# A decode-attention kernel: masks filled by GpSimd, and the output projection in column blocks of 64

## The chip, the cores and the metric

The kernel runs on one core of a Trainium2 chip. The core has a matrix engine (TensorE, "PE" in the profile; "PEld" is its weight loading), a vector engine (VectorE, "DVE"), an activation engine (ScalarE, "ACT"), a general engine (GpSimd, "POOL"), and a queue engine (SyncE, "SP") that issues most transfers. Sixteen DMA engines carry the transfers. The metric is the device time of one execution in microseconds; smaller is better.

## The reference

One decode step for eight sequences (B = 8, one new token each, D = 512):

```python
xn = layernorm(x)
q = (xn @ wq)                         # 32 heads of 128
k = k_cache[:, :, Sk - W:, :]         # 8 key/value heads, window W = 1024 of 4096
v = v_cache[:, :, Sk - W:, :]         # each shared by 4 query heads
p = softmax(q @ k^T * 128**-0.5)
s = (p @ v).reshape(8, 1, 4096) @ wo  # 4096 -> 512
g = silu((gelu(xn @ w_gate) * (xn @ w_up)) @ w_down)   # F = 1792
out = x + s * g
```

All inputs are bfloat16. The windows of the two caches are 16.8 MB each, wq and wo 4.2 MB each, and the three feed-forward matrices 1.8 MB each: about 47 MB are read once, and 8 KB are written.

## The kernel before

The kernel is written in an order fixed by hand; each engine works through its instructions in program order and waits on semaphores for others.

Loads. Nearly all go through SyncE's queue in one order: wq in three pieces, the gate and up matrices, keys and values of the eight heads alternately (K three heads ahead), the down matrix among them, and at the end wo in five pieces. They land in a pool of nine large buffers (`big`), so that a load is issued when the buffer it takes has been read by its last reader. A cache load of one head is 2 MB. wo comes as `pieces`: row blocks m = 0 and 1 together, m = 2, then m = 3 in three cuts of 4, 3 and 1 row groups.

Start. GpSimd fills identity matrices and zeroed tiles (`zeros`, `quarter`, `sums`, `oL`, L156 to L248). The new tokens are normalised, the query projection runs (L305), and the queries are turned. `spread_x` puts x into the layout of the output. The gate and up products follow (L355), and between them `masks()` builds four masks on VectorE from the identity matrix: `parts` and `gsel` by reductions; `own`, the score mask read by L461; `same`, read by L477; and `sums`, the row-summing weights of L541.

Attention. For each of 16 sets s (a head and half of the sequences) there are steps spread over the loop: transposition of keys by TensorE (L431) with copies out of PSUM by VectorE (L442) and ScalarE (L444), the scores (L453), masking and maxima (L461, L472, L477), exponentials (L486), a turn of the probabilities (L493), and the product with the values (L519). For each head, `gather` (L541) sums the partial rows and `divide` (L550, L553) normalises; for each pair of heads, `turn_pair` (L568) transposes the result into `oL`. The steps of the feed-forward part are put between them; `fold` and `gate` end it.

Output. A transposed pair m holds 8 row groups r. The 512 output columns are cut into blocks; `spread` and `project` compute block q = NG * s + g into partition group g of a PSUM tile (partitions 32g to 32g + 31), and they shift the weights by s columns so that row b * NS2 + s of that group holds sequence b. With NG = 2 and NS2 = 2 there are four blocks of 128 columns. `oL` has a row pitch of `OL + 1`, and a read shifted by s takes its place from that odd pitch. Since a head's result holds each sequence PB = 4 times, `turn_pair` writes four copies of a pair; with NS2 = 2 a pair owns two of the places, and the other two lie in the places of the next pair, which writes them anew later.

End. Two VectorE operations multiply by the gate and add x (L675, L676); two stores, one from ScalarE's queue (L680) and one from SyncE's (L681), write the 8 KB of output.

Of the kernel before, what the change touches and what calls it, by code (L numbers as in the profile page):

```python
# [11 lines left out]
BF16 = mybir.dt.bfloat16  # L12
FP32 = mybir.dt.float32
# [4 lines left out]
def kernel(  # L18
# [13 lines left out]
    nc = tc.nc  # L32

    B, Sq, D = A_x.shape
    Hkv, Sk, Dh = A_k_cache.shape[1], A_k_cache.shape[2], A_k_cache.shape[3]
# [8 lines left out]
    P = nc.NUM_PARTITIONS  # L44
# [17 lines left out]
    NQB = D // 128  # L62
    PB = 32 // B

    NG = 2
    NS2 = NQB // NG
    NEG = -1.0e30


# [5 lines left out]
    small = ctx.enter_context(tc.tile_pool(name="small", bufs=3))  # L75
    rows = ctx.enter_context(tc.tile_pool(name="rows", bufs=1))
# [4 lines left out]
    ps_s = ctx.enter_context(tc.tile_pool(name="ps_s", bufs=1, space=PSUM))  # L81
# [6 lines left out]
    m_top = m_ps[:, 0:P]  # L88
# [3 lines left out]
    x_sb = rows.tile([B, D], BF16, name="x_sb")  # L92
# [48 lines left out]
    for k0, cuts in ((0, (1, 1)), (2, (2,))):  # L141
        t = big.tile([P, 2, Hq * Dh], BF16, name="big")
        i = 0
        for n in cuts:
            nc.sync.dma_start(  # L145
                out=t[:, i : i + n, :],
                in_=A_wq.rearrange("(p k) n -> p k n", p=P)[:, k0 + i : k0 + i + n, :],
# [10 lines left out]
    def select(out, in_, op, fill, base, pattern, cm):  # L158
# [8 lines left out]

    sizes = (2 * NS * 2 * NC, NDC * 32, NDC * 32, 32 + NS2)
    zeros = rows.tile([P, sum(sizes)], BF16, name="zeros")
# [16 lines left out]
        out=xhat, in0=x_sb, scalar1=mv[:, 0:1], scalar2=rstd[:, 0:1],  # L186
# [6 lines left out]
    for k in range(NDC):  # L193
# [4 lines left out]
        out=xqT.rearrange("p k (y g) f -> p k g y f", y=NB)[:, :, :, :, 0],  # L198
        in_=xnT_ps.rearrange("p k (g y) -> p k g y", y=NB),
# [10 lines left out]

    sel = sel0[0:B]
    nc.vector.tensor_copy(out=sel[:, NS2 : NS2 + B * NS2 : NS2], in_=ident[0:B, 0:B])
    xf = rows.tile([32 * NG, 128], FP32, name="xf")

    def spread(ps, first, src):

        for g in range(NG):
            for s in range(NS2):
                q = NG * s + g
                nc.tensor.matmul(  # L220
                    ps[32 * g : 32 * g + 32, :], first[:, NS2 - s : NS2 - s + 32],
                    src[:, q * 128 : (q + 1) * 128],
                    start=(s == 0), stop=(s == NS2 - 1), skip_group_check=True,
                )

    def spread_x():
        spread(m_top, sel, x_sb)
        nc.vector.tensor_copy(out=xf, in_=m_top[0 : 32 * NG])

# [4 lines left out]
    half = lead.tile([P, 2], FP32, name="half")  # L236
    quarter = consts.tile([P, NS2 + 32], FP32, name="quarter")
    nc.gpsimd.memset(quarter, 0.0)
# [2 lines left out]
    nc.gpsimd.memset(sums, 0.0)  # L241
    qT = qT0.rearrange("p (e s c g j) -> p e s c g j", e=2, c=2, g=G, j=rep)


    OW = 32
    OL = R8 * OW
    oL = rows.tile([P, NS2 * (Hkv // 2 + 1), OL + 1], BF16, name="oL")
    nc.gpsimd.memset(oL, 0.0)  # L248

    def masks():  # L250
        nc.vector.tensor_reduce(
            out=parts, in_=identf.rearrange("p (x n) -> p n x", n=NC),
            axis=AX.X, op=ALU.max,
        )
        nc.vector.tensor_reduce(
            out=gsel, in_=parts.rearrange("p (g j) -> p g j", j=rep),
            axis=AX.X, op=ALU.max,
        )
        nc.vector.tensor_reduce(
            out=half, in_=identf.rearrange("p (r c n) -> p c r n", c=2, n=NC),  # L260
            axis=AX.XY, op=ALU.max,
        )
        nc.vector.tensor_reduce(
            out=quarter[:, NS2 : NS2 + B * NS2 : NS2],
            in_=identf.rearrange("p (a b f) -> p f b a", b=B, f=PB)[:, 0],
            axis=AX.X, op=ALU.max,
        )

        nc.vector.tensor_scalar(
            out=gsel, in0=gsel, scalar1=-1.0, scalar2=-NEG, op0=ALU.add, op1=ALU.mult  # L270
        )
        nc.vector.tensor_copy(
            out=own.rearrange("p c b g -> p (c b) g"),
            in_=gsel.unsqueeze(1).to_broadcast([P, CP * 32 // G, G]),
        )

        m = small.tile([P, NC], FP32, name="m16")
        nc.vector.tensor_scalar(
            out=m, in0=parts, scalar1=-1.0, scalar2=-NEG, op0=ALU.add, op1=ALU.mult
        )  # L280
        nc.vector.tensor_copy(
            out=same, in_=m.unsqueeze(1).to_broadcast([P, NR * 2, NC])
        )
        for b in range(NB):
            for a in range(2):
                nc.vector.tensor_copy(
                    out=sums[:, b, a].rearrange("p j (g y) f -> p y j g f", y=NB)[:, b],
                    in_=parts.rearrange("p (g j a) -> p a j g", a=2, g=G)[:, a]
                    .unsqueeze(3).to_broadcast([P, rep // 2, G, PB]),
                )  # L290

    hT = rows.tile([P, NFC, 32], BF16, name="hT")
    g_sb = rows.tile([32 * NG, 128], FP32, name="g_sb")

# [3 lines left out]
    for k in range(NDC):  # L300
        w = wq_rows[k]
# [11 lines left out]
    for c in range(2):  # L313
        nc.vector.tensor_copy(  # L314
            out=q_row[:, 0, :, :, c, :],
            in_=q_ps[0].rearrange("p (j w e) -> p j e w", j=rep, e=2),
        )
        nc.scalar.activation(  # L318
            out=q_row[:, 1, :, :, c, :],
            in_=q_ps[1].rearrange("p (j w e) -> p j e w", j=rep, e=2),  # L320
# [25 lines left out]
    FG = F // NQB  # L346
    zu = [ps_s.tile([P, FG], FP32, name="s"), ps_o.tile([P, FG], FP32, name="o_ps")]
    spread_x()
    KW = NDC
    for w, src in enumerate((B_w_gate, B_w_up)):  # L350
        for k0 in range(0, NDC, KW):
            wt = load_rows(src, k0, KW, NDC, "gu")
            for k in range(KW):
                for g in range(NQB):
                    nc.tensor.matmul(  # L355
                        zu[w][32 * g : 32 * g + 32, :], xn(k0 + k),
                        wt[:, k, g * FG : (g + 1) * FG],
                        start=(k0 + k == 0), stop=(k0 + k == NDC - 1),
                        skip_group_check=True,
                    )  # L360
            if w == 0 and k0 == 0:
                for t in range(NT):
                    turn_queries(t)
                masks()
# [8 lines left out]
            out=z2, in0=z2, scalar1=0.044715, scalar2=1.0, op0=ALU.mult, op1=ALU.add  # L373
# [3 lines left out]
            out=z2, in_=z2, func=ACT.Tanh, scale=0.7978845608028654  # L377
        ),
        lambda: nc.vector.tensor_scalar(
            out=z2, in0=z2, scalar1=0.5, scalar2=0.5, op0=ALU.mult, op1=ALU.add  # L380
# [3 lines left out]
            out=h_row.rearrange("p j i -> p i j"),  # L384
# [4 lines left out]
            out=hT.rearrange("p j r -> p (j r)"), in_=h_row.rearrange("p j i -> p (j i)")  # L389
# [3 lines left out]
    f_state = {}  # L393
# [14 lines left out]
    def fold():  # L408


        f_sb = rows.tile([P, 2 * NT * HD], BF16, name="q_row")[:, 0 : 2 * D].bitcast(FP32)
        nc.scalar.activation(out=f_sb, in_=f_state["ps"], func=ACT.Copy)
        spread(m_top, quarter, f_sb)
        f_state["ps"] = m_top[0 : 32 * NG]

    def gate():
        f_ps = f_state["ps"]
        th = small.tile([32 * NG, 128], FP32, name="th", bufs=1)
        nc.scalar.activation(out=th, in_=f_ps, func=ACT.Tanh, scale=0.5)
        nc.vector.tensor_scalar(  # L420
            out=th, in0=th, scalar1=0.5, scalar2=0.5, op0=ALU.mult, op1=ALU.add
        )
        nc.vector.tensor_tensor(out=g_sb, in0=th, in1=f_ps, op=ALU.mult)
# [182 lines left out]
    for t in range(end + 4):  # L606
        s, i = divmod(t, 2)
# [30 lines left out]
        if t == LV + 1:  # L638
            fold()
            gate()  # L640
# [4 lines left out]
            value_half(s3, i3)  # L645


    s_ps = ps_s.tile([32 * NG, 128], FP32, name="s")

    def project(m, r, w):  # L650
        t = oL[:, NS2 * m : NS2 * (m + 1)].rearrange("p f y -> p (f y)")
        for s in range(NS2):
            a = s * OL + r * OW
            for g in range(NG):
                q = NG * s + g
                nc.tensor.matmul(  # L656
                    s_ps[32 * g : 32 * g + 32, :], t[:, a : a + OW],
                    w[:, q * 128 : (q + 1) * 128],
                    start=(m == 0 and r == 0 and s == 0),
                    stop=(m == Hkv // 2 - 1 and r == R8 - 1 and s == NS2 - 1),  # L660
                    skip_group_check=True,
                )
# [5 lines left out]
    for m0, r0, nr, nm in pieces:  # L668
        t = load_wo(m0, r0, nr, nm)
        for m in range(m0, m0 + nm):  # L670
            for r in range(r0, r0 + nr):
                project(m, r, t[m - m0][:, r - r0, :])
    tmp = small.tile([32 * NG, 128], FP32, name="tmp", bufs=1)
    out_sb = small.tile([32 * NG, 128], BF16, name="out_sb", bufs=1)
    nc.vector.tensor_tensor(out=tmp, in0=s_ps, in1=g_sb, op=ALU.mult)  # L675
    nc.vector.tensor_tensor(out=out_sb, in0=tmp, in1=xf, op=ALU.add)  # L676
    rows_out = out.flatten_outer_dims().rearrange(
# [34 lines left out]
```

## Time and profile before

| | before |
|---|---|
| median of 3 runs | 120.65 us (120.53 to 120.98) |
| the profiled execution's own time | 120.78 us |
| its span, first to last instruction | 118.7 us |
| mean granted TensorE clock | 0.936 |
| busy: TensorE, VectorE, ScalarE, GpSimd | 87.9, 68.4, 55.6, 4.6 us |
| read from memory | 47.46 MB, 400 GB/s over the span |

The span is counted from the first to the last instruction of the program; the timed execution has some more around it. A line of a group reads: line, engine, operation, tile written and tiles read, shapes, count; then busy time, mean duration in ns, and the engine's idle time before, with what ended it. L656 is line 656 of the kernel before. In a timeline a row gives the start and the duration in microseconds. "SPq" is SyncE's queue, "PEq" the sequencer of TensorE. The slices cut the span into 40 equal parts, and each digit is a busy share in tenths.

### The profile page before, as it was taken

The page shows a single profiled execution, that of the slowest core. Times are in us where ns is not written, and L with a number is a line of the kernel's source. Part 1 is how long each engine was busy: PE and PEld are TensorE (multiplying, and loading weights), DVE is VectorE, ACT ScalarE, POOL GpSimd, SP SyncE. Part 2 cuts the span into 40 slices and gives each one's busy share as a digit, 9 for nine tenths or more (in the row PEclk, how much of TensorE's full clock was granted, in tenths as well). Part 3 has the DMA queues.
Part 4 walks back from the last instruction along what each step waited for, and adds up shares of the span by engine and source line. Part 5 has one row for each costly group of instructions (what it writes and reads, how often), then busy time and mean ns, then how long its engine had stood idle before and what let it go on. Part 6 is the DMA issues. An engine that isn't in the chain of part 4 may idle for free.

```text
span 118.7 us, 2373 instructions
## 1 busy us (share of the span) xinstructions
PE 87.9 (74%) x974; PEld 61.4 (52%) x974; DVE 68.4 (58%) x179; ACT 55.6 (47%) x94; POOL 4.6 (4%) x12
## 2 busy tenths in 40 slices
PE   0070629599482999687996799999499989499770
PEld 0020216197352677375674467776385766278660
DVE  1310131827799766668488149988445997538801
ACT  0500030239808667578388138849605866424000
POOL 7700000000000000000000000000000000000000
PEclk9999999999999589999999679999958999959997
DMA  3999999999999999999999999999999999999940
GB/s 102 422 450 436 406 444 419 419 433 428 417 459 409 426 419 430 419 425 430 425 425 425 425 433 428 417 430 430 425 425 425 430 417 436 422 422 430 411 153 3
DMA packets 6186, 47.60 MB, mean 401 GB/s; under 512 B 537, under 2 KB 673, under 8 KB 929
## 3 DMA queue, kind: packets, MB, share of 16 engines
q1 hardware_dynamic: 6128, 47.45, 95.0%
q8 instruction: 7, 0.11, 0.3%
q10 hardware_dynamic: 48, 0.01, 0.0%
q14 instruction: 3, 0.02, 0.0%
HBM read 47.46 MB, written 0.01 MB: 400 GB/s over the span
## 4 chain that ended last, share of the span: by engine, by line
DMA 89%; SPq 6%; PE 1%; DVE 0%; issue 0%
DMA big<-in_A_v_cache_dram 54%; DMA big<-in_A_wo_dram 20%; DMA big<-in_A_k_cache_dram 15%; SPq L135 4%; SPq L145 1%; SPq L99 1%; PE s L656 1%; PE kT_ps L431 1%; PE s L519 0%; DVE tmp L675 0%; DVE out_sb L676 0%
## 5 line engine op out<-in xcount | busy, mean ns | idle before, releaser
L444 ACT ACTIVATE kT<-kT_ps 128x1024 bf16<-128x1024 bf16 x32 | 32.5, 1022 | 26.1 <-PE kT_ps L431 25.6
L431 PE MATMUL kT_ps<-identf,big 128*128 128x128 f32 x256 | 39.8, 303 | 0.8 <-DMA big<-in_A_k_cache_dram 0.7
L431 PEld LDWEIGHTS kT_ps<-identf,big 128*128 128x128 f32 x256 | 31.2, 154 | 9.8 <-PE sc L453 2.5
L442 DVE COPY kT<-kT_ps 128x1024 bf16<-128x1024 bf16 x32 | 22.4, 700 | 11.6 <-PE kT_ps L431 10.9
L461 DVE CUSTOM_DVE_ANT_0 sc_sb<-sc,own 128x512 f32<-128x512 f32 x16 | 10.7, 669 | 6.3 <-PE sc L453 6.3
L486 ACT ACTIVATE p<-sc_sb,bias 128x512 bf16<-128x512 f32 x16 | 11.4, 715 | 5.6 <-DVE bias L477 5.6
L493 DVE STREAM_TRANSPOSE pT<-p 128x512 bf16<-128x512 bf16 x16 | 11.2, 702 | 2.7 <-ACT p L486 2.7
L519 PEld LDWEIGHTS <-pT 128*32 128x32 bf16 x256 | 6.5, 99 | 9.7 <-issue 5.4
L472 PE MATMUL m_ps<-identf,top 128*128 128x128 f32 x32 | 6.9, 297 | 5.7 <-DVE top L461 5.7
L453 PE MATMUL sc<-kT,zeros 128*32 128x512 bf16 x128 | 10.5, 407 | 0.6 <-ACT kT L444 0.6
L541 PE MATMUL m_ps<-blk,sums 128*64 128x129 f32 x64 | 10.9, 336 | 0.1
L541 PEld LDWEIGHTS m_ps<-blk,sums 128*64 128x64 f32 x64 | 8.6, 169 | 1.8 <-issue 1.0
L472 PEld LDWEIGHTS m_ps<-identf,top 128*128 128x128 f32 x32 | 4.8, 190 | 7.1 <-DVE top L461 7.0
L519 PE MATMUL s<-big,pT 128*32 128x256 bf16 x80 | 4.2, 286 | 4.5 <-DMA big<-in_A_v_cache_dram 4.5
L519 PE MATMUL o_ps<-big,pT 128*32 128x256 bf16 x112 | 5.9, 274 | 0.4 <-DVE blk L502 0.4
L305 PE MATMUL sc<-big,zeros 128*32 128x512 bf16 x16 | 2.5, 611 | 4.7 <-DMA big<-in_A_wq_dram 4.2
L314 DVE CAST q_row<-sc 128x512 bf16<-128x512 f32 x2 | 1.3, 686 | 7.9 <-PE sc L305 7.9
L656 PE MATMUL s<-big,oL 128*32 128x128 bf16 x128 | 4.3, 219 | 1.3 <-DMA big<-in_A_wo_dram 1.3
L568 DVE STREAM_TRANSPOSE oL<-o 128x256 bf16<-128x256 bf16 x4 | 5.3, 1313 | 0.0
L477 DVE CUSTOM_DVE_ANT_0 scr<-m_ps,same 128x128 f32<-128x128 f32 x16 | 4.5, 280 | 0.6 <-PE m_ps L472 0.6
L318 ACT ACTIVATE q_row<-o_ps 128x512 bf16<-128x512 f32 x2 | 1.1, 594 | 8.0 <-PE o_ps L305 8.0
L656 PEld LDWEIGHTS <-oL 128*32 128x32 bf16 x128 | 3.8, 96 | 1.9 <-issue 1.9
(76 smaller groups left out, 63.0 us busy)
## 6 DMA issues: line engine op xcount, KB each, us to landing
big<-in_A_k_cache_dram SPq DMA_DIRECT2D x7, 2048.0 KB, 34.0
big<-in_A_v_cache_dram SPq DMA_DIRECT2D x7, 2048.0 KB, 33.2
big<-in_A_wq_dram SPq DMA_DIRECT2D x2, 1024.0 KB, 5.8
big<-in_A_wq_dram SPq DMA_DIRECT2D x1, 2048.0 KB, 11.2
big<-in_A_k_cache_dram SPq DMA_DIRECT2D x2, 1024.0 KB, 21.4
big<-in_A_v_cache_dram SPq DMA_DIRECT2D x2, 1024.0 KB, 30.4
big<-in_A_wo_dram SPq DMA_DIRECT2D x1, 2048.0 KB, 30.9
big<-in_B_w_gate_dram SPq DMA_DIRECT2D x1, 1792.0 KB, 15.0
```

The costliest lines, as they stand in the source:

```text
L431: nc.tensor.transpose(ps[:, c, :], K[s][:, 2 * (i * QP + c) : 2 * (i * QP + c) + 2, :] .rearrange("p c d -> p (c d)").bitcast(FP32), identf,)
L442: nc.vector.tensor_copy(out=out, in_=in_)
L444: nc.scalar.activation(out=out, in_=in_, func=ACT.Copy)
L453: nc.tensor.matmul(ps[32 * R : 32 * R + 32], qT[:, e, s].rearrange("p c b j -> p (c b j)"), t[:, :, 32 * R : 32 * R + 32, e], start=(e == ...
L461: nc.vector.tensor_tensor_reduce(out=sc[s], in0=ps.rearrange("p c k -> p (c k)"), in1=own.rearrange("p c b g -> p (c b g)"), op0=ALU.add, ...
L472: nc.tensor.matmul(ps, top.pop(s).to_broadcast([P, P]), identf, start=True, stop=True)
L486: nc.scalar.activation(out=P_[s], in_=sc.pop(s), func=ACT.Exp, scale=scale, bias=biases.pop(s), accum_out=blk[s][:, Dh : Dh + 1],)
L493: nc.vector.transpose(out=pT[s].rearrange("p c k -> p (c k)"), in_=P_.pop(s))
L519: nc.tensor.matmul(o_ps[s][32 * q : 32 * q + 32].rearrange("p c d -> p (c d)"), pT[s][:, c, :], V[s][:, 2 * c : 2 * c + 2, :].rearrange("p ...
L541: nc.tensor.matmul(m_out[64 * x : 64 * x + 64, a, :], sums[:, b, a].rearrange("p j b f -> p (j b f)"), t[b], start=(b == 0), stop=(b == NB ...
L568: nc.vector.transpose(out=out[:, :, 0 : B * NS2 : NS2, :], in_=o_pair.pop(h).rearrange("p r a d -> p (r a d)"),)
L656: nc.tensor.matmul(s_ps[32 * g : 32 * g + 32, :], t[:, a : a + OW], w[:, q * 128 : (q + 1) * 128], start=(m == 0 and r == 0 and s == 0), s ...
```

## The change

`NS2` goes from 2 to 4 and a block of output columns from 128 to 64 (`DQ`), with two column groups as before; the eight blocks are spread over rows b * 4 + s. So x and the gate are laid out in 32 rows of 64 columns per group, a projection step has eight matmuls of 64 columns instead of four of 128, a pair owns all four copies in `oL` (which grows from 10 to 16 places), the copies are written with a stride of 4 elements rather than 2, and each store has 32 runs of 128 bytes instead of 16 of 256. In `masks()` the four reductions stay on VectorE; the eight operations that fill `own`, `same` and `sums` go to GpSimd.

```diff
     NG = 2
-    NS2 = NQB // NG
+    NS2 = PB
+    DQ = D // (NG * NS2)
...
-    xf = rows.tile([32 * NG, 128], FP32, name="xf")
+    xf = rows.tile([32 * NG, DQ], FP32, name="xf")
...
     def spread(ps, first, src):
...
                 nc.tensor.matmul(
                     ps[32 * g : 32 * g + 32, :], first[:, NS2 - s : NS2 - s + 32],
-                    src[:, q * 128 : (q + 1) * 128],
+                    src[:, q * DQ : (q + 1) * DQ],
...
     def spread_x():
-        spread(m_top, sel, x_sb)
-        nc.vector.tensor_copy(out=xf, in_=m_top[0 : 32 * NG])
+        spread(m_top[:, 0:DQ], sel, x_sb)
+        nc.vector.tensor_copy(out=xf, in_=m_top[0 : 32 * NG, 0:DQ])
...
-    oL = rows.tile([P, NS2 * (Hkv // 2 + 1), OL + 1], BF16, name="oL")
+    oL = rows.tile([P, NS2 * Hkv // 2, OL + 1], BF16, name="oL")
     nc.gpsimd.memset(oL, 0.0)
...
-        nc.vector.tensor_scalar(
+        nc.gpsimd.tensor_scalar(
             out=gsel, in0=gsel, scalar1=-1.0, scalar2=-NEG, op0=ALU.add, op1=ALU.mult
         )
-        nc.vector.tensor_copy(
+        nc.gpsimd.tensor_copy(
             out=own.rearrange("p c b g -> p (c b) g"),
...
-        nc.vector.tensor_scalar(
+        nc.gpsimd.tensor_scalar(
             out=m, in0=parts, scalar1=-1.0, scalar2=-NEG, op0=ALU.add, op1=ALU.mult
         )
-        nc.vector.tensor_copy(
+        nc.gpsimd.tensor_copy(
             out=same, in_=m.unsqueeze(1).to_broadcast([P, NR * 2, NC])
         )
         for b in range(NB):
             for a in range(2):
-                nc.vector.tensor_copy(
+                nc.gpsimd.tensor_copy(
                     out=sums[:, b, a].rearrange("p j (g y) f -> p y j g f", y=NB)[:, b],
...
-    g_sb = rows.tile([32 * NG, 128], FP32, name="g_sb")
+    g_sb = rows.tile([32 * NG, DQ], FP32, name="g_sb")
...
-        spread(m_top, quarter, f_sb)
-        f_state["ps"] = m_top[0 : 32 * NG]
+        spread(m_top[:, 0:DQ], quarter, f_sb)
+        f_state["ps"] = m_top[0 : 32 * NG, 0:DQ]
...
-        th = small.tile([32 * NG, 128], FP32, name="th", bufs=1)
+        th = small.tile([32 * NG, DQ], FP32, name="th", bufs=1)
...
-    s_ps = ps_s.tile([32 * NG, 128], FP32, name="s")
+    s_ps = ps_s.tile([32 * NG, DQ], FP32, name="s")
...
                 nc.tensor.matmul(
                     s_ps[32 * g : 32 * g + 32, :], t[:, a : a + OW],
-                    w[:, q * 128 : (q + 1) * 128],
+                    w[:, q * DQ : (q + 1) * DQ],
...
-    tmp = small.tile([32 * NG, 128], FP32, name="tmp", bufs=1)
-    out_sb = small.tile([32 * NG, 128], BF16, name="out_sb", bufs=1)
+    tmp = small.tile([32 * NG, DQ], FP32, name="tmp", bufs=1)
+    out_sb = small.tile([32 * NG, DQ], BF16, name="out_sb", bufs=1)
```

## The prediction

> **What bounds the kernel now.** I read the page first: the slices of DMA and TensorE, then the chain that ended last.
>
> ```profile
> span 118.7 us, 2373 instructions
> PE   0070629599482999687996799999499989499770
> DMA  3999999999999999999999999999999999999940
> GB/s 102 422 450 436 406 444 419 419 433 428 417 459 409 426 419 430 419 425 430 425 425 425 425 433 428 417 430 430 425 425 425 430 417 436 422 422 430 411 153 3
> DMA 89%; SPq 6%; PE 1%; DVE 0%; issue 0%
> ```
>
> The DMA engines are full from the second slice to the third from last, at some 425 GB/s, and 89% of the chain is transfers. TensorE's slices reach 9 here and there, but the chain holds 1% of it. So the first 115 us are the loads' time, and an engine counts there only if it frees a buffer so late that the queue runs dry. The table of DMA issues puts the landing of a cache load 33 to 34 us after its issue: that much is queued ahead.
>
> Next the chain in order of time, and the instructions in order of time from 108 us on (start, duration, what, idle time before it):
>
> ```profile
> 91.22 23.78 DMA big<-in_A_wo_dram
> 115.00 0.04 issue
> 115.04 0.64 PE s L656 x16
> 115.67 0.02 issue
> 115.70 0.29 DVE tmp L675
> 115.99 0.02 issue
> 116.02 0.28 DVE out_sb L676
> ```
>
> ```profile
> 110.35 1.96 PE L656 MATMUL s<-big,oL 128*32 128x128 bf16 x64 [0.31 <-DMA big<-in_A_wo_dram]
> 111.03 1.31 DVE L568 STREAM_TRANSPOSE oL<-o 128x256 bf16<-128x256 bf16 x1
> 112.80 1.07 PE L656 MATMUL s<-big,oL 128*32 128x128 bf16 x32 [0.49 <-DMA big<-in_A_wo_dram]
> 114.10 0.62 PE L656 MATMUL s<-big,oL 128*32 128x128 bf16 x16 [0.23 <-DMA big<-in_A_wo_dram]
> 115.04 0.62 PE L656 MATMUL s<-big,oL 128*32 128x128 bf16 x16 [0.31 <-DMA big<-in_A_wo_dram]
> 116.33 0.36 SPq L681 DMA_DIRECT2D out_dram<-out_sb  x1
> ```
>
> Before each of the four groups of output-projection matmuls TensorE waits for its piece of A_wo, 0.23 to 0.49 us. Only what stands behind the last landing (115.00) is surely on the path: 16 matmuls, two VectorE operations, the store (1.4 and 1.5 us from issue to landing) and the program's end. But the earlier waits are short, and this is the number to keep: TensorE has 4.69 us, from 110.35 to 115.04, for everything but the last 16 matmuls.
>
> **The change, step by step.** The sum is made against the profiled execution: 118.7 us of span, 120.78 us as timed, so 2.1 us outside the span. It lies 0.13 us above the median of the three runs, 120.65.
>
> *Output projection (L656).* 128 matmuls of 128 columns become 256 of 64, in the same two column groups, each still with its own weight load of 32 columns. The pace now: 64 matmuls in 1.96 us, less the last one's 0.22, over 63 steps, is 27.6 ns. Sorting all starts of the trace, no 16 in a row come closer than 27.2 ns: the value products of L519, 256 columns over four groups, four in 109 ns. Two matmuls of 128 in 55.2 and four of 256 in 108.8 lie on one line, 0.42 ns per column plus 1.6, so both are paced by columns streaming in parallel groups. By that line two of 64 take 28.4 ns, 14.2 each: this is the low end. What sets a pace for shorter matmuls the trace hardly shows. The four transposes of 8 columns (L194) fill 0.29 us with 0.17 for the last, 40 ns per step in one group; two such groups side by side would give 20 ns each, in file 40 ns, the far end. For overlap speaks the start of a scores group, where four matmuls and four loads of different column groups begin within 15 ns:
>
> ```profile
> 28.88:28.89 0.01, 0.01 (x4) 0.01 (x4) 1.00 0.00 0
> ```
>
> (a window of L453 alone; TensorE busy and its instructions, weight loads busy and theirs, clock 1.00.) I take 14.2, from the same line of code and the same groups. The last 32 then take 31 x 14.2 ns plus 0.19 for one, 0.63 us, against 0.62: +0.01. At 20 ns it is 0.81, +0.19, still without a backlog (128 x 20 ns ends at 112.91, the next 64 at 114.19, the next 32 before 115.04). Above 20.9 ns per matmul (224 of them in 4.69 us) backlog forms; that is the first rival.
>
> [...]
>
> *Last VectorE operations (L675, L676).* 64x128 becomes 64x64. The rows give 0.28 us for 128 columns and 0.61 for 448 (L375): 1.03 ns per column, so -0.066 each, -0.13 together, wholly on the path.
>
> *Store.* Each of the two issues goes from 16 runs of 256 bytes to 32 of 128, the same 4 KB. The issue takes 0.36 us here and 0.42 for a wq load over 128 rows: under 0.01 more. The packets of both stores lie within 0.2 us in the DMA slices; if twice the runs took twice that it would be +0.2; if bytes decide, 0. I take +0.05, nearer the low end, since most of the 1.4 us is before and after the packets.
>
> *Masks on GpSimd.* Eight operations leave VectorE, 1.4 us from 22.39 on, and VectorE then idles 1.27 us for a key transpose anyway: no gain.
>
> ```profile
> 22.39 0.16 DVE L269 TENSOR_SCALAR gsel<-gsel 128x4 f32<-128x4 f32 x1
> 22.59 0.43 DVE L272 COPY own<-gsel 128x512 f32<-128x512 f32 x1
> 24.97 0.69 DVE L442 COPY kT<-kT_ps 128x1024 bf16<-128x1024 bf16 x1 [1.27 <-PE kT_ps L431]
> 31.44 0.68 DVE L461 CUSTOM_DVE_ANT_0 sc_sb<-sc,own 128x512 f32<-128x512 f32 x1
> L248 POOL MEMSET oL<- 128x2570 bf16 x1 | 2.2, 2240 | 0.0
> ```
>
> GpSimd copies stand nowhere in this trace. Its fills go at 0.87 ns per element (2.24 us for 2570), its selects take 0.29 us for 128: own about 0.5 us, same 0.3, six small ones 0.1 each, 1.4 us in all; four times that, 5.6 us, is my far end. They start when gsel is reduced, 22.17, and end between 23.6 and 27.8. What waits for them is L461 at 31.44, with a key copy (L442) and the gated product (L383) queued behind it on VectorE and the maxima of L472 waiting for it; then L477 at 35.4, and on TensorE the row sums (L541) at 57: no cost. Without that cover a delay would still have to use up the 33 us of queued loads. The larger oL fill (4112 columns, 3.6 us by the same rate) ends near 6.5 instead of 5.2; GpSimd's next work is at 22.2 and oL's first writer at 76.3: nothing.
>
> *Turned pairs (L568).* The transposition already writes four copies, two of which the next pair overwrites; now all four stay and the stride is 4, not 2. It reads and writes as many elements, 1.31 us. Were it half or double, the last one would end at 111.7 or 113.7 (with the one before it doubled too, 115.0); its 64 readers start at 114.10. Taken as nothing; at worst they start at 115.0 in one run, 63 x 14.2 ns plus 0.19, and end 0.4 later than now.
>
> *Spreading x and the gate (L220).* Four more matmuls at 14.7 us, before a 2.2 us wait for the gate weights, and four at 49.6, under the queued loads; four VectorE and ScalarE operations get shorter there. Nothing. The SyncE queue keeps its order, so no load moves.
>
> The sum: +0.01 - 0.13 + 0.05 = -0.07, so 120.78 - 0.07 = 120.7 us.
>
> **Rivals.**
>
> *TensorE's pace does not rise with shorter matmuls (slower).* Place: L656, 110.35 to the end. At today's 27.6 ns the first 128 end at 113.88, the next 64 at 115.65, the next 32 at 116.53, and the last at 117.58 instead of 115.66: +1.92, less 0.13, plus 0.05, is +1.84, 122.6 us. At 40 ns it would be +5. It decides from 20.9 ns on. For it: no stretch of the trace is faster than 27.2 ns per load and matmul. Against it: both fast stretches are explained by columns alone, and different groups start within a few ns. Chance 0.27. [...]
>
> *The store of short runs (slower).* Should the landing grow by half, 0.7 us, the time is 121.4. For it: the whole end waits on it; no store of such runs is in the trace. Against: the packets are 0.2 of the 1.4 us. Chance 0.05.
>
> *The masks come late (slower).* They would need over 9 us, six times my estimate, and then outlast the queued loads; one stall of 1 us would show as about 121.7. Chance 0.02.
>
> *Faster by over 0.5%.* The tail can give only 0.13 us, so the loads themselves would have to end 0.5 us earlier, 120.0. For it: a few slices reach 450 GB/s. Against: no load changes size, order or release. Chance 0.06.
>
> *Nothing of note*, the forecast: 0.60.
>
> **The numbers.** About 0.5% (0.6 us) is what can be told from no change here; the three runs span 0.45 us. Forecast 120.7; its own range is 120.4 (no cost but the shorter VectorE work, and a run as quick as the quickest) to 121.15 (20 ns per matmul and the dearer store). Beyond it the first rival weighs most: to leave out no more than 2 in 10 the range goes up to 122.7, about the middle of that rival, and from 120.3 below. Faster 0.06, same 0.60, slower 0.27 + 0.05 + 0.02 = 0.34.
>
> **What the profile would show.** Right: L656 with 256 matmuls at 14 to 20 ns, still waiting for A_wo before each group; the last DVE operations at 0.22; the stores landing in 1.4 to 1.6 us; GpSimd's copies over before 28 us, no wait for POOL at L461; the last A_wo landing near 115.0. Wrong: waits for A_wo gone from L656 and TensorE unbroken from 110.35; or a store landing above 1.9 us; or digits below 9 in the DMA slices ahead of 110 us.

## The result, and the profile after

| | before | changed |
|---|---|---|
| median | 120.82 us (120.53 to 120.98, 6 runs) | 121.86 us (121.51 to 122.08, 6 runs) |
| profiled span | 118.7 us | 120.1 us |
| ratio, changed to before | | 1.009, 95% interval 1.0076 to 1.0103 |

The change costs 0.9%, some 1.04 us. That lies in the stated range, but it is not the case I forecast: I had expected nothing of note. In the experiments below, one run of four fewer (122.93 us, granted clock 0.93, the others 0.954 to 0.986) and one of 254 more (122.80 us, 0.929, the others 0.957 to 1.0) had a lower clock than the rest and are left out of the ratios.

The slices, and the end of the chain in order of time (start, duration, what), of the changed kernel:

```profile
DMA  3999999999999999999999999999999999999810
115.06 0.04 issue
115.10 0.63 PE s L656 x31
115.73 1.22 issue
116.95 0.22 PE s L656
117.17 0.02 issue
117.19 0.23 DVE tmp L675
117.42 0.02 issue
117.44 0.22 DVE out_sb L676
```

The loads end where they ended: the last piece of A_wo lands at 115.06, against 115.00. Then comes one new row, "115.73 1.22 issue". TensorE has finished 255 of the 256 output matmuls and waits 1.22 us before the last, for nothing that the profile shows: no semaphore, no transfer of data, no other engine. Everything behind it is moved by as much. The output matmuls end at 117.17 instead of 115.67, 1.5 us later; the two VectorE operations give back 0.12 us; the span is 1.4 us longer.

The instructions of the output part in order of time (changed kernel) show a second stop of the same kind:

```profile
108.72 0.09 PEld L656 LDWEIGHTS <-oL 128*32 128x32 bf16 x1 [0.17 <-issue]
110.43 2.03 PE L656 MATMUL s<-big,oL 128*32 128x64 bf16 x127 [1.63 <-DMA big<-in_A_wo_dram]
113.22 1.60 PE L656 MATMUL s<-big,oL 128*32 128x64 bf16 x97 [0.77 <-issue]
115.10 0.63 PE L656 MATMUL s<-big,oL 128*32 128x64 bf16 x31 [0.28 <-DMA big<-in_A_wo_dram]
116.95 0.20 PE L656 MATMUL s<-big,oL 128*32 128x64 bf16 x1 [1.22 <-issue]
117.69 0.36 SPq L681 DMA_DIRECT2D out_dram<-out_sb  x1
```

The stops stand before the 128th and the 256th matmul. Each matmul comes with a weight load, so they are exactly 256 instructions apart. And the DMA queues, in the stretch from 110.4 to 117.2 us of the changed kernel, hold two packets of a kind that moves no data of the kernel (count, MB, share of the 16 engines); the kernel before, from 110.4 to 115.7 us, holds one:

```profile
q8 instruction: 2, 0.03, 2.0%
q8 instruction: 1, 0.02, 1.0%
```

The two are 16 KB each, start at 110.94 and 114.34, and there are eight such packets over the span, against seven before. I took them for TensorE's program, fetched in blocks of 16 KB, of 256 instructions by the distance of the stops. That gave the theory for the experiments. **Code blocks:** the fetch of a block starts only when TensorE has begun the block before it; the output part now runs through two blocks in less time than two fetches take, and its last matmul happens to be the first instruction pair of a new block. Two rivals: **short matmuls**, something in the stream of 64-column matmuls itself that stalls its end; and **masks**, the work moved to GpSimd.

### The profile page after: what moved, and what is told of

It reads as the page before. It is cut to its first block, busy times and chain, and to the rows that moved or that the text cites. A ratio compares the mean times of both kernels' runs of the same rounds, so it can differ in the third digit from the quotient of the medians.

```text
span 120.1 us, 2654 instructions
## 1 busy us (share of the span) xinstructions
PE 84.6 (70%) x1114; PEld 58.1 (48%) x1114; DVE 67.5 (56%) x171; ACT 55.6 (46%) x94; POOL 7.8 (6%) x20
## 4 chain that ended last, share of the span: by engine, by line
DMA 84%; PE 7%; SPq 3%; issue 2%; DVE 1%
DMA big<-in_A_v_cache_dram 54%; DMA big<-in_A_wo_dram 20%; DMA big<-in_A_wq_dram 9%; PE kT_ps L431 3%; SPq L136 2%; PE o_ps L519 1%; PE m_ps L541 1%; PE sc L453 1%; PE s L656 1%; SPq L146 1%; PE m_ps L221 1%; DVE kT L442 1%; PE s L519 0%; DVE blk L502 0%; DVE tmp L675 0%
## 5 line engine op out<-in xcount | busy, mean ns | idle before, releaser
L431 PE MATMUL kT_ps<-identf,big 128*128 128x128 f32 x256 | 38.1, 293 | 2.6 <-DMA big<-in_A_k_cache_dram 2.5
L431 PEld LDWEIGHTS kT_ps<-identf,big 128*128 128x128 f32 x256 | 29.4, 148 | 11.8 <-issue 4.9
L461 DVE CUSTOM_DVE_ANT_0 sc_sb<-sc,own 128x512 f32<-128x512 f32 x16 | 10.7, 669 | 6.2 <-PE sc L453 6.2
L453 PE MATMUL sc<-kT,zeros 128*32 128x512 bf16 x128 | 11.2, 428 | 0.6 <-ACT kT L444 0.6
L541 PE MATMUL m_ps<-blk,sums 128*64 128x129 f32 x64 | 8.7, 290 | 0.3 <-DVE o L553 0.3
L541 PEld LDWEIGHTS m_ps<-blk,sums 128*64 128x64 f32 x64 | 6.8, 141 | 1.8 <-issue 0.8
L656 PE MATMUL s<-big,oL 128*32 128x64 bf16 x256 | 4.5, 193 | 3.9 <-issue 2.0
L656 PEld LDWEIGHTS <-oL 128*32 128x32 bf16 x256 | 4.1, 97 | 4.4 <-issue 4.4
```

Source lines behind the costliest of these rows:

```text
L431: nc.tensor.transpose(ps[:, c, :], K[s][:, 2 * (i * QP + c) : 2 * (i * QP + c) + 2, :] .rearrange("p c d -> p (c d)").bitcast(FP32), identf,)
L453: nc.tensor.matmul(ps[32 * R : 32 * R + 32], qT[:, e, s].rearrange("p c b j -> p (c b j)"), t[:, :, 32 * R : 32 * R + 32, e], start=(e == ...
L461: nc.vector.tensor_tensor_reduce(out=sc[s], in0=ps.rearrange("p c k -> p (c k)"), in1=own.rearrange("p c b g -> p (c b g)"), op0=ALU.add, ...
L541: nc.tensor.matmul(m_out[64 * x : 64 * x + 64, a, :], sums[:, b, a].rearrange("p j b f -> p (j b f)"), t[b], start=(b == 0), stop=(b == NB ...
L656: nc.tensor.matmul(s_ps[32 * g : 32 * g + 32, :], t[:, a : a + OW], w[:, q * DQ : (q + 1) * DQ], start=(m == 0 and r == 0 and s == 0), sto ...
```

## The experiments

### Four instructions fewer, 24 more, 128 more, and the masks back

Four kernels on one chip, each compared with the kernel before on that chip; the changed kernel itself was not run again, and its ratio to before, 1.009, is what theirs are set against. `spread_x` is the place for changes to the length of TensorE's program: it stands at 14.7 us, ahead of a wait of 2 us for the gate weights, far from the end.

Four fewer leaves out the last block of x (s = 3) in both column groups, so a quarter of the output lacks x. In the diffs here and below, the loops inside `spread` that follow its new argument are left out:

```diff
     def spread_x():
-        spread(m_top[:, 0:DQ], sel, x_sb)
+        spread(m_top[:, 0:DQ], sel, x_sb, NS2 - 1)
```

> The changed kernel with the last block of x left out of spread_x (one quarter of the output rows lacks x): two matmuls and two weight loads fewer on TensorE at 14.7 us, nothing else. Theory (code blocks): TensorE's program comes in blocks of 256 instructions, each fetched only when the block before it has begun; in the changed kernel the 256th output matmul is the first one of a new block and waits 1.22 us for it. With four instructions fewer it moves into the block before: the wait before the last matmul is gone, the output matmuls end near 115.75, span 118.7, time 120.4 to 120.7. Rival (short matmuls): something of the stream of 64-column matmuls itself stalls its end; then the wait stays before the last matmul and the time at 121.9. Rival (masks on GpSimd): no change either, 121.9.

Measured: 120.63 us median, ratio to before 1.0002 (0.9975 to 1.0029). Eight of the ten runs lie at 120.39 to 120.70. The other two took 122.93 and 122.09, and the expectation did not have the latter. The profile is of the run at 122.93 and is not used, so that the wait is gone from a quick execution of this kernel is seen in its time alone. Two matmuls with their loads less at 14.7 us, where TensorE waits anyway, gave back 1.2 us.

The masks back on VectorE, with TensorE's program untouched:

```diff
-        nc.gpsimd.tensor_scalar(
+        nc.vector.tensor_scalar(
...
-                nc.gpsimd.tensor_copy(
+                nc.vector.tensor_copy(
```

> The changed kernel with the eight mask operations back on VectorE; TensorE's program is the same instruction for instruction. Code blocks: no difference to the changed kernel, 121.9 within 0.3, the wait of about 1.2 us before the last output matmul stays. Rival (masks on GpSimd cost the time): back to 120.8. Rival (short matmuls): 121.9.

Measured: 122.02 us (121.92 to 122.18), ratio to before 1.0114 (1.0097 to 1.0131). The stop is where it was, by the timeline of this kernel:

```profile
115.02 0.63 PE L656 MATMUL s<-big,oL 128*32 128x64 bf16 x31 [0.27 <-DMA big<-in_A_wo_dram]
116.87 0.20 PE L656 MATMUL s<-big,oL 128*32 128x64 bf16 x1 [1.22 <-issue]
```

The masks theory falls: they cost nothing on GpSimd, and nothing comes back without them there.

24 more instructions in the kernel before, which keeps its matmuls of 128 columns. It has 280 TensorE instructions fewer than the changed kernel; 24 more bring its last matmul to the same place in a block, 256 short of it:

```diff
-        spread(m_top, sel, x_sb)
+        for _ in range(4):
+            spread(m_top, sel, x_sb)
```

> The kernel before, with the four matmuls of spread_x done four times instead of once (same result): 24 more TensorE instructions at 14.7 us, under the wait for the gate weights. Code blocks: the last output matmul, of 128 columns, now stands first in a new block, which is asked for when the block before it begins, at about 110.0, and is ready 4 to 5.5 us later: 114.5 to 115.9, where the matmul wants to start at 115.44. Between no change and 0.5 us slower, 120.8 to 121.3, with a wait for issue before the last output matmul if the time moves. Rival (short matmuls): 120.8, no wait before the last matmul. Rival (masks): 120.8.

Measured: 121.16 us (120.81 to 122.16, 10 runs), ratio 1.0047 (1.0022 to 1.0072). Slower, as expected of code blocks and not of the rivals. But the runs scatter, three of ten at 121.65 to 122.16, and the profile was of the quickest, 120.81, in which nothing waits.

128 more instructions in the changed kernel:

```diff
-        spread(m_top[:, 0:DQ], sel, x_sb)
+        for _ in range(9):
+            spread(m_top[:, 0:DQ], sel, x_sb)
```

> The changed kernel with spread_x's eight matmuls done nine times (same result): 128 more TensorE instructions at 14.7 us. Code blocks: the block border moves to 64 matmuls before the end and the one before it to 192 before the end; the wait before the last matmul goes, a wait for issue stands before the last 64 (at about 114, until 115.0 to 115.9), which then run in 0.93 us without waiting for A_wo; the end of the output matmuls is 116.2 to 117.0 against 117.17 now, time 121.0 to 121.8. Rival (short matmuls): the wait stays before the last matmul, 121.9. Rival (masks): 121.9.

Measured: 122.09 us (121.60 to 122.15), ratio 1.0107 (1.0086 to 1.0127), 0.3 above the expected span of times. The stop has moved as it should (timeline; the helper lines stand one further down in this kernel, L657 for L656):

```profile
110.33 2.04 PE L657 MATMUL s<-big,oL 128*32 128x64 bf16 x128 [1.66 <-DMA big<-in_A_wo_dram]
112.77 1.09 PE L657 MATMUL s<-big,oL 128*32 128x64 bf16 x63 [0.39 <-DMA big<-in_A_wo_dram]
115.89 1.14 PE L657 MATMUL s<-big,oL 128*32 128x64 bf16 x65 [2.03 <-issue]
```

It stands now after 191 matmuls, with 65 left, where 128 instructions more put a border 64 matmuls earlier; the last 65 run through without a stop, past the landing of the last A_wo. Code blocks had said after 192. A stop whose place is set by instructions 99 us earlier is none of the output matmuls' own: the short-matmul theory falls too.

### Two fewer, 254 more, 22 more

If only the place within a block counts, two instructions fewer must do as much as four, and 254 more, a whole block less two, must do the same.

```diff
-        spread(m_top[:, 0:DQ], sel, x_sb)
+        spread(m_top[:, 0:DQ], sel, x_sb, ((1, NS2 - 1),))
```

(The new argument names what is left out, here group 1, s = 3; an eighth of the output lacks x.)

> The changed kernel with one matmul and its weight load left out of spread_x (one eighth of the output rows lacks x): two TensorE instructions fewer. Code blocks: the last output matmul is now the last of its block, and the first output weight load (at 108.7, ahead of the wait for A_wo) the first of the block two before, so the fetch of the next block is asked for as early as in the changed kernel, and not only after the wait at 110.3 as with four fewer. No wait before the last matmul in any run: 120.4 to 120.7, and none of the runs near 122 that four fewer had. A wait for issue until about 113.2 stays, after 128 matmuls instead of 127, and costs nothing. Rival (the place of blocks does not matter, four fewer gained by something else): 121.9, or the same spread of times as four fewer.

```diff
     def spread_x():
+        for _ in range(15):
+            spread(m_top[:, 0:DQ], sel, x_sb)
+        spread(m_top[:, 0:DQ], sel, x_sb, ((1, NS2 - 1),))
         spread(m_top[:, 0:DQ], sel, x_sb)
```

> The changed kernel with 127 more matmuls and weight loads in spread_x (same result): 254 more TensorE instructions at 14.7 us, which is one whole block of 256 less two. Code blocks: the borders at the end fall as with two fewer, so 254 more instructions make the changed kernel faster: 120.4 to 120.9, below the 122.1 of 128 more, with no wait before the last matmul. Rival (more instructions always cost, by fetches or by TensorE's time): 122 or above.

Measured: 254 more, 120.62 us median (12 runs), ratio to before 1.002 (0.9988 to 1.0052); seven runs lie at 120.26 to 120.71, four at 121.69 to 122.00, one at 122.80. Two fewer, 121.28 us (10 runs, 120.21 to 121.79), ratio 1.0028 (0.9998 to 1.0058); four runs at 120.21 to 120.55, six at 121.22 to 121.79. So adding 254 instructions did make the changed kernel faster, by 1.2 us at the median (a ratio to before of 1.002 against 1.009), and the quick runs of both lie where they were expected, or up to 0.2 us below. The expectation for two fewer held for these four runs alone: that none would lie near 122 was wrong, and six of its ten are 0.5 us or more above its range. The profiles show both kinds of execution. Of 254 more, a quick execution (timeline):

```profile
110.45 2.04 PE L661 MATMUL s<-big,oL 128*32 128x64 bf16 x128 [1.87 <-DMA big<-in_A_wo_dram]
113.31 2.36 PE L661 MATMUL s<-big,oL 128*32 128x64 bf16 x128 [0.82 <-DMA big<-in_A_wo_dram]
```

and of two fewer, one at 121.33:

```profile
110.29 2.04 PE L658 MATMUL s<-big,oL 128*32 128x64 bf16 x128 [0.28 <-DMA big<-in_A_wo_dram]
114.55 2.04 PE L658 MATMUL s<-big,oL 128*32 128x64 bf16 x128 [2.21 <-issue]
```

In neither does anything stand before the last matmul. Both stop after 128, at the other border; but one goes on at 113.31, and then still waits for the last A_wo, while the other goes on at 114.55 and ends late. (The profile puts the 113.31 down to a landing; but the weight load just ahead of that matmul, which reads nothing of A_wo, starts no sooner.) What differs is when the block before began. Its first instruction is the first weight load of the output part, at 108.51 in the one and 109.94 in the other. From the traces' records, in us (the start of the first weight load of a block, counted back from the stops; the start of the code packet that follows; the start of the next block's first weight load):

```
kernel              block begins   next code packet   next block begins
changed                  108.41             110.94              113.22
masks on VectorE         108.30             110.73              113.14
254 more                 108.51             110.97              113.31
two fewer                109.94             112.16              114.54
128 more                 111.23             113.63              115.89
changed, last block      113.22             114.34              116.95
```

While the loads run, a block is ready 4.6 to 4.8 us after the block before it has begun; at the end, as the loads run out, 3.7 us. And what makes the begin early or late, in these profiles, is the granted clock shortly before, when the row sums run (windows: stretch, us, TensorE busy and instructions, granted clock, DMA share, GB/s), of two fewer:

```profile
104.00:106.00 2.00, 2.00 (x14) 0.50 1.04 438
106.00:108.00 2.00, 2.00 (x54) 0.70 1.00 426
```

of 254 more:

```profile
104.00:106.00 2.00, 2.00 (x48) 1.00 1.00 422
106.00:108.00 2.00, 1.73 (x39) 1.00 1.04 442
```

At half clock the sums (L541) end 1.4 us later, and the output part begins later. The other profiles with a border at this place agree. That of 22 more and two of the three of 24 more have a stretch of 3.4 us at half clock earlier, between 96.5 and 100.4 us, and there the block begins at 109.75 to 110.19; the changed kernel, masks on VectorE, 254 more and the third profile of 24 more have no such stretch between 81 and 108 us, and there it begins at 108.23 to 108.51. In the kernel before, the dip (0.50 from 104 to 106 us in its profile) costs nothing: its last border stands before the last 117 matmuls, and the packet of that block had started at 101.68. This reading rests on the profiles of eight executions and the one before; why the clock dips in some of them, and whether the long runs without a profile had such a dip, was not looked into.

The mirror of it, 22 more in the kernel before, two less than 24:

```diff
-        spread(m_top, sel, x_sb)
+        for skip in ((), (), ((1, NS2 - 1),), ()):
+            spread(m_top, sel, x_sb, skip)
```

> The kernel before with 11 more matmuls and weight loads in spread_x (same result): 22 more TensorE instructions, two fewer than in the run with 24 more. Code blocks: the last output matmul is the last of its block, so nothing waits: 120.7 to 120.9 in every run, and none of the runs near 122 that 24 more had. Rival (padding itself costs): as with 24 more, a median of 121.2 and some runs near 122.

Measured: 120.87 us (120.54 to 121.57, 10 runs), ratio 1.0016 (1.0001 to 1.0031). Nine runs lie at 120.54 to 121.11, one at 121.57, none near 122; three of the ten lie within the 120.7 to 120.9 that were expected of all. The interval still overlaps that of 24 more, so this alone would be weak; it points the way that code blocks say.

### 24 more, twice again

No profile had shown one of the longer executions of 24 more.

> The kernel before with 24 more TensorE instructions again, to see a profile of one of its longer executions (3 of 10 were near 122.1, and the profile was of one at 120.8). Code blocks: an execution near 122 shows TensorE waiting for issue before the last output matmul, until about 116.8, and the code packet of that block starting after 114; one near 120.9 shows the packet at 112 to 113 and no wait. Rival (the longer executions have another cause, such as later loads of A_wo): an execution near 122 shows the output matmuls complete within 0.7 us of the last landing, later than 115.

> The same kernel a third time, with the same expectations: near 122 with a wait for issue before the last output matmul, or near 120.9 without one.

Measured: 120.72 and 120.63 us beside 120.79 of the kernel before, both without a wait before the last matmul. No longer execution was caught. The records do show where the border stands. In the three profiles of 24 more a further code packet starts at 119.74, 119.68 and 119.30 us, 4.0 to 4.4 us after the weight load of the last output matmul, and 22 more has none so late: with 24 more that matmul opens a block, with 22 more it does not. The block's own packet starts at 110.80 to 112.29 there, so that by the 2.3 to 2.6 us of the table it is ready by 114.9 at the latest, before the matmul's turn at 115.2 to 115.4; hence no wait. That the longer executions of 24 more wait for code is likely from the other kernels, but not shown, and the border alone does not foretell 1.3 us for them.

## Why the prediction was wrong in its likeliest case

What held, by its own steps. The pace of the short matmuls: 127 in 2.03 us are 14.6 ns each, where I took 14.2 from the line through two rows; 31 of the last 32 run in the 0.63 us that I gave to all. VectorE's end: 0.23 and 0.22 us by the chain, -0.12 against -0.13. The store: 0.36 us to issue, 1.4 and 1.5 us to landing, as before; I had +0.05, near nothing. The turned pairs: 1.30 and 1.32 us at the end, unchanged. The masks are done by 24.45 us, and L461 starts without a wait for GpSimd, earlier than before, at 30.30:

```profile
22.60 0.61 POOL L272 COPY own<-gsel 128x512 f32<-128x512 f32 x1
23.56 0.29 POOL L281 COPY same<-m 128x128 f32<-128x128 f32 x1
23.79 0.66 POOL L286 COPY sums<-parts 128x32 f32<-128x32 f32 x4
30.30 0.68 DVE L461 CUSTOM_DVE_ANT_0 sc_sb<-sc,own 128x512 f32<-128x512 f32 x1
```

The step that failed is "the last 32 then take 31 x 14.2 ns plus 0.19 for one", the +0.01 of the sum. It counted the matmuls as if their instructions were always there. 256 instructions more in the output part, and 24 more in the spreading that I costed "nothing" (8 for x and 16 for the gate, where the trace has eight matmuls more and I had counted four), have a price of their own: the code comes by DMA, a block at a time, and in the table above a block took 3.7 to 4.8 us to be ready. In its place the runs show 1.22 us of waiting before one matmul, +1.5 us at the end of the output part.

The first rival named the right place and direction: TensorE cannot take its instructions faster in the output part. Its mechanism was wrong, and its +1.84 us too large for the 1.04 measured. It was a pace per matmul, at 27.6 ns for each, and the pace is 14.6. That 121.86 lies in the range is luck: the range was widened upward for this rival, and the cause that I found was in none of the rivals. Nor did it stand among the signs: those named as right came, except that of the four waits for A_wo two were left, and a wait for issue stood in the place of the other two; of those named as wrong none came. What is limited is the supply of blocks: 256 instructions, 128 matmuls with their loads, in 3.7 to 4.8 us, 29 to 38 ns per matmul where a stretch is long enough to need two blocks. A weight load and a matmul take 14.6 ns together, so 128 of each, a block, are used up in 1.9 us, about half the 3.7 us in which the last block was ready, and the wait is 1.22 us.

The profile before held the signs: the count "q8 instruction: 7" and the trace's records, in which 1.9 to 3.1 us pass from the begin of each of the last four blocks to the packet of the next. I read the queue table for its bytes, 0.11 MB, and not for its latency.

## What to carry to other kernels

When a change doubles the number of TensorE's instructions in a short, fast stretch, count them in blocks of 256 and ask when each block is asked for; here a block was ready 4.6 to 4.8 us after the one before it had begun while the DMA engines were full (share 0.99 from 110.4 to 113.1 us of the changed kernel). Other engines were not looked at. "Issue" before an instruction that waits for nothing else, at places 256 instructions apart, is the sign. It is cheap to test: a few more or fewer harmless instructions far ahead move the stop, and four instructions were worth 0.9% here, so a small difference between two kernels may come from where a border falls and not from what was changed.

## What had not been expected of the hardware

The packet is the smaller part of a fetch. It takes 0.88 to 0.97 us in the traces of the two kernels (1.26 for the changed kernel's last, at 114.34), but in the table it starts 2.2 to 2.5 us after the block before has begun while loads run (1.1 us at the end), and the first instruction of the block follows another 2.3 to 2.6 us after the packet's start. Elsewhere in these two traces, where no stop shows the border, the first of these two times was not fixed: 1.2 to 6.1 us. And two groups of 32 columns with matmuls of 64 columns each keep a pace of 14.6 ns per weight load and matmul (127 in 2.03 us).
